# Attention forward and backward with a K/V cache: preparations moved inside the pair loop, the second phase's first operands loaded early, narrower blocks

## The chip, the cores and the metric

The kernel runs on one core of one Trainium2 chip. The time is device microseconds of that core for one execution. Comparisons are always with runs of the kernel before on the same chip in the same rounds.

The engines' short names in the profile: PE is the matmul engine (TensorE), PEld its weight loads, DVE, ACT and POOL are VectorE, ScalarE and GpSimd, SP is SyncE, which here only issues DMAs.

## The reference

```python
B, Sq, D = 16, 112, 448
H, Sk, Dh = 16, 512, 256

def _fwd_reference(x, k_cache, v_cache, wq, wo):
    q = (x @ wq).reshape(B, Sq, H, Dh).transpose(0, 2, 1, 3)
    scores = jnp.einsum("bhqd,bhkd->bhqk", q, k_cache) * (Dh ** -0.5)
    p = softmax(scores, axis=-1)
    o = jnp.einsum("bhqk,bhkd->bhqd", p, v_cache)
    return o.transpose(0, 2, 1, 3).reshape(B, Sq, H * Dh) @ wo

def reference(x, k_cache, v_cache, wq, wo, grad_out):
    out, vjp = jax.vjp(_fwd_reference, x, k_cache, v_cache, wq, wo)
    return (out, *vjp(grad_out))        # out, dx, dk_cache, dv_cache, dwq, dwo
```

All arrays are bf16. (The random inputs are cut, and the transposes are written out plainly.)

## The kernel before

Phase 1 goes over 128 pairs of heads (16 batches of 8 pairs) in a software pipeline: an iteration does the first half of pair `a` and the rest of pair `bb = a - 1`. It writes dV and dK, and it leaves O and dQ in two DRAM tiles, the stash. Phase 2a reads the stash in blocks of 512 columns for dWo (`out_5`) and dWq (`out_4`); phase 2b reads it again, transposed, in 14 chunks of rows for out and dx.

```python
    o_stash = dram.tile([B * SQ, HD], bf, name="o_stash")
    dq_stash = dram.tile([B * SQ, HD], bf, name="dq_stash")
    # ...
    def w_prep(hp):               # Wo of one pair of heads, transposed; first batch only
        # ... 2 x 8 transposes on PE, each half followed by
            nc.vector.tensor_copy(WoT_sb[...], pb[:DCH, :].rearrange(...))      # L105
    def b_prep(b):                # x and grad of one batch, transposed
        # ... 4 + 4 transposes on PE
        nc.vector.tensor_copy(xgT[:]..., pb[:DCH, :2 * DC * SQ])                # L130
    # ...
    for per in range(NPAIR + 1):
        a, bb = per, per - 1
        A, Bv = valid(a), valid(bb)
        # ... loads of K and V of the next pair
        if A:
            s_dOproj(a)           # its first matmul (L178) reads WoT_sb and xgT
            s_Qproj(a); s_T(a); s_QdT(a)
        if Bv:
            s_dV(bb); s_dST(bb)
        if A:
            s_S(a); s_dP(a)       # softmax; dP; dS on POOL
        if Bv:
            s_dK(bb); s_O(bb); s_dQ(bb)     # the last two write the stash
        if A:
            s_PT(a)
        if A:
            ba, hpa = pair_bh(a)
            if ba == 0 and hpa + 1 < HP:
                w_prep(hpa + 1)             # for the next pair
            if hpa == HP - 1 and ba + 1 < B:
                b_prep(ba + 1)              # for the next pair
    mctx.close()                  # phase 1's memory comes free
    # ... phase 2a
    load_rows(g_all, g_flat, 0, D, nc.sync)
    for blk in range(HD // 512):
        Ot = ph2.tile([P, NCH, 512], bf, name="Ot")
        load_rows(Ot, o_stash, blk * 512, (blk + 1) * 512, nc.sync)
        if blk == 0:
            load_rows(x_all, x_flat, 0, D, nc.sync)
        dQt = ph2.tile([P, NCH, 512], bf, name="dQt")
        load_rows(dQt, dq_stash, blk * 512, (blk + 1) * 512, nc.sync)
        if blk == 0:
            nc.sync.dma_start(Wo_nat[:], ...)           # 3.7 MB in one DMA
        # ... 4 groups x 14 matmuls with Ot (L436), 4 x 14 with dQt (L449)
    nc.sync.dma_start_transpose(WqT[:], wq)             # all of Wq in one DMA
    for ch, (r0, rn) in enumerate(chunks):              # phase 2b
        # ... transposed loads of the stash's rows; 32 matmuls L467, 32 of L471
    store_rows(out_flat, res_out, nc.sync)              # 1568 KB each, at the end
    store_rows(dx_flat, res_dx, nc.scalar)
```

## Time and profile before

| | before |
|---|---|
| median of 6 runs (range) | 1710.83 us (1708.72 to 1715.4) |
| span of the profiled run, PE's mean granted clock | 1710.0 us, 0.995 |
| PE busy | 1652.5 us, 97% |
| one ordinary pair / one pair that ends a batch | 9.93 us / 11.83 us |
| PE's first matmul of phase 2 | 1348.52 us |
| end of PE's last matmul | 1702.2 us |

PE is the bound, so the first view to read is the list of its waits; the prediction below shows it. A listed wait runs from the recorded end of PE's previous matmul to the start of the next. This is one batch boundary in the timeline of the kernel before (start, duration, engine, line, operation, out<-in; the two lines after these, the copy of L130 and L178, stand in the prediction):

```profile
1004.63 0.37 PE L127 MATMUL bankb<-ident_bf,g_sb 112*112 112x112 bf16 x4
...
1005.05 0.69 DVE L248 TENSOR_TENSOR O_sb<-bank,rinv 112x512 bf16<-112x512 f32 x1
```

L178 starts at 1006.32, after a listed wait of 1.32 us. Between the transposes and the copy that PE waits for stands DVE's evacuation of O.

### The profile page before, as it was taken

Reading aid. Unit: us, or ns where it says so; the run is one execution under the profiler, and the core shown is the slowest. Engines: PE = TensorE matmul, PEld = TensorE weight load, DVE = VectorE, ACT = ScalarE, POOL = GpSimd, SP = SyncE. Lnnn points to the kernel's source line nnn. Section 1 sums busy time; section 2 is a strip of 40 time slices with the busy share of each in tenths; the row PEclk is TensorE's granted clock in tenths of the full one; section 3 lists DMA queues with packets and bytes.
Section 4 is the critical chain, followed back from the end, with each engine's and each line's share of the span. In section 5 each row is a group of like instructions: output and inputs, shape, how many; then the busy total and the mean of one; then the engine's idle time right before and its main releaser. Section 6 shows DMA issues by size and latency. Waiting matters only on the chain.

```text
span 1710.0 us, 33740 instructions
## 1 busy us (share of the span) xinstructions
PE 1652.5 (97%) x11776; PEld 1271.6 (74%) x11776; DVE 968.3 (57%) x1870; ACT 979.0 (57%) x2095; POOL 719.9 (42%) x854
## 2 busy tenths in 40 slices
PE   7999999999999999999999999999999699999998
PEld 5778888888888888888888888888888455555554
DVE  4767677677676776777767777676777211110000
ACT  3667777777777777777777777777767210100000
POOL 4445554455544555445554455554555111110000
PEclk9999999999999999999999999999999899999999
DMA  9767797867776667677776667776666997618885
GB/s 261 235 220 235 241 278 237 267 228 241 229 237 230 233 229 239 229 234 229 229 239 232 232 227 238 232 238 225 231 228 225 347 317 245 213 39 172 172 173 149
DMA packets 356474, 390.40 MB, mean 228 GB/s; under 512 B 148464, under 2 KB 221728, under 8 KB 356304
## 3 DMA queue, kind: packets, MB, share of 16 engines
q1 hardware_dynamic: 348640, 371.96, 69.7%
q0 software_dynamic: 4864, 13.77, 2.5%
q10 hardware_dynamic: 2800, 2.52, 0.5%
q8 instruction: 93, 1.52, 0.4%
q14 instruction: 77, 0.63, 0.1%
HBM read 181.01 MB, written 174.13 MB: 208 GB/s over the span
## 4 chain that ended last, share of the span: by engine, by line
PE 88%; DVE 4%; issue 3%; DMA 2%; ACT 1%; POOL 1%; SPq 0%; POOLq 0%; ACTq 0%
PE bank L161 13%; PE bank L178 7%; PE bank L189 6%; PE bank L283 6%; PE bank L214 6%; PE bank L259 6%; PE bank L449 6%; PE bank L300 5%; PE bank L245 5%; PE bank L326 5%; PE bank L436 5%; PE bank L471 5%; PE bank L467 5%; PE bank L315 2%; PE bank L234 2%
## 5 line engine op out<-in xcount | busy, mean ns | idle before, releaser
L224 POOL TENSOR_SCALAR Pn<-Pu,rinv 112x512 bf16<-112x512 bf16 x256 | 173.8, 691 | 600.5 <-DVE rinv L221 591.2
L267 POOL TENSOR_TENSOR dS<-tmp,t 112x512 bf16<-112x512 f32 x256 | 325.8, 1273 | 21.2
L168 DVE COPY VT<-bank 128x512 f32<-128x512 f32 x128 | 88.5, 691 | 231.8 <-PE bank L161 231.8
L219 ACT ACTIVATE Pu<-bank,nmax 112x512 bf16<-112x512 f32 x256 | 173.5, 682 | 71.8 <-DVE nmax L217 71.7
L305 DVE CAST dk_sb<-bank 128x512 bf16<-128x512 f32 x256 | 172.8, 681 | 70.7 <-ACT Pu L219 69.9
L263 DVE CUSTOM_DVE_ANT_0 tmp<-bank,Pn 112x512 f32<-112x512 f32 x256 | 173.7, 691 | 38.9 <-POOL Pn L224 38.7
L265 POOL TENSOR_SCALAR t<-Pn,Dv 112x512 f32<-112x512 bf16 x256 | 177.1, 692 | 20.5 <-DVE Dv L263 20.1
L192 ACT ACTIVATE Q_sb<-bank 112x512 bf16<-112x512 f32 x128 | 76.4, 597 | 190.4 <-PE bank L189 190.4
L288 DVE CAST dv_sb<-bank 128x512 bf16<-128x512 f32 x256 | 165.0, 685 | 17.3 <-DMA out_dram<-dv_sb 0.8
L217 DVE TENSOR_REDUCE nmax<-bank 112x1 f32<-112x512 f32 x256 | 165.0, 686 | 1.9 <-PE bank L214 1.9
L178 PE MATMUL bank<-WoT_sb,xgT 112*112 112x512 bf16 x512 | 134.1, 382 | 25.8 <-DVE xgT L130 20.6
L161 PE MATMUL bank<-ident_f,v 128*128 128x128 f32 x1024 | 154.8, 274 | 2.0 <-DMA v<-in_v_cache_dram 2.0
L161 PE MATMUL bank<-ident_f,k 128*128 128x128 f32 x1024 | 154.8, 273 | 0.7 <-DMA k<-in_k_cache_dram 0.7
L166 ACT COPY KT<-bank 128x512 f32<-128x512 f32 x256 | 152.2, 595 | 2.0 <-PE bank L161 1.4
L161 PEld LDWEIGHTS bank<-ident_f,k 128*128 128x128 f32 x1024 | 124.6, 141 | 22.1 <-issue 1.5
L286 ACT CAST dv_sb<-bank 128x512 bf16<-128x512 f32 x256 | 138.8, 599 | 0.7 <-DMA out_dram<-dv_sb 0.6
L214 PE MATMUL bank<-KT,QdT 128*112 128x512 bf16 x512 | 137.6, 390 | 0.6 <-ACT QdT L204 0.6
L259 PE MATMUL bank<-VT,QdT 128*112 128x512 bf16 x512 | 136.9, 388 | 0.0
L303 ACT CAST dk_sb<-bank 128x512 bf16<-128x512 f32 x256 | 136.7, 592 | 0.0
L329 ACT ACTIVATE dQ_sb<-bank 112x512 bf16<-112x512 f32 x128 | 76.4, 597 | 100.3 <-PE bank L326 98.6
L189 PE MATMUL bank<-Wq_sb,xgT 112*112 112x512 bf16 x512 | 133.2, 381 | 0.0
L245 PE MATMUL bank<-v,PT 128*112 128x256 bf16 x1024 | 133.0, 272 | 0.2 <-ACT Pu L219 0.2
(64 smaller groups left out, 2879.9 us busy)
## 6 DMA issues: line engine op xcount, KB each, us to landing
k<-in_k_cache_dram SPq DMA_DIRECT2D x128, 512.0 KB, 3.9
v<-in_v_cache_dram SPq DMA_DIRECT2D x128, 512.0 KB, 4.5
out_dram<-dv_sb SPq DMA_DIRECT2D x256, 256.0 KB, 2.3
out_dram<-dk_sb SPq DMA_DIRECT2D x256, 256.0 KB, 2.3
o_stash<-O_sb SPq DMA_DIRECT2D x128, 112.0 KB, 3.0
dq_stash<-dQ_sb SPq DMA_DIRECT2D x128, 112.0 KB, 2.9
Ot<-o_stash SPq DMA_DIRECT2D x8, 1792.0 KB, 9.2
dQt<-dq_stash SPq DMA_DIRECT2D x8, 1792.0 KB, 9.3
```

The source lines that it names most:

```text
L161: nc.tensor.transpose(ps[:, s * P:(s + 1) * P], src[:, hh, s, :].bitcast(f32), ident_f[:])
L178: nc.tensor.matmul(ps_do[:SQ, :], xgT[:, 1, c, :], WoT_sb[:, c, h0 * DH:(h0 + 2) * DH], start=(c == 0), stop=(c == DC - 1))
L189: nc.tensor.matmul(ps_q[:SQ, :], xgT[:, 0, c, :], Wq_sb[:, c, h0 * DH:(h0 + 2) * DH], start=(c == 0), stop=(c == DC - 1))
L214: nc.tensor.matmul(ps_s[:SQ, :], st.QdT[:, hh, e::2], st.KT[hh][:, e::2], start=(e == 0), stop=(e == 1))
L219: nc.scalar.activation(Pu[:], ps_s[:SQ, :], ACT.Exp, bias=nmax[:], scale=1.0, accum_out=rs[:, hh:hh + 1])
L224: nc.gpsimd.tensor_scalar(Pn[:], st.Pu[hh][:], st.rinv[:, hh:hh + 1], 1.0, ALU.mult, ALU.mult)
L245: nc.tensor.matmul(ps_o[:SQ, hh * DH:(hh + 1) * DH], st.PT[:, hh * 2 + t, e2::2], st.v2[:, hh, s, :], start=(s == 0), stop=(s == NS - 1))
L259: nc.tensor.matmul(ps_dp[:SQ, :], st.QdT[:, 2 + hh, e::2], st.VT[hh][:, e::2], start=(e == 0), stop=(e == 1))
L263: nc.vector.tensor_tensor_reduce(tmp[:], ps_dp[:SQ, :], st.Pn[hh][:], 1.0, 0.0, ALU.mult, ALU.add, Dv[:])
L265: nc.gpsimd.tensor_scalar(t2[:], st.Pn[hh][:], Dv[:], -1.0, ALU.mult, ALU.mult)
L267: nc.gpsimd.tensor_tensor(dS_t[:], tmp[:], t2[:], op=ALU.add)
L305: nc.vector.tensor_copy(dk_sb[:, 2:4, :].rearrange("p s d -> p (s d)"), ps[:])
```

## The change

Its intent: PE should not wait at the batch boundaries, in the first batch, or between the phases, and the last stores should be short.

1. `b_prep` and `w_prep` move from the end of the iteration to just after the Q/dO transposes.
2. The stash is split into a tile with the rows of the first 14 batches and one with those of the last 2. x, grad and the first block's operands get memory of their own and are loaded before phase 1 ends; the first block of phase 2a works on 12 full chunks of rows first.
3. Phase 2a has one block of 512 columns and 14 of 256. Wq's transpose and Wo come in four pieces each, in blocks 3 to 10. SP's order of issues in phase 2 is as written (`manual_schedule`); before, the scheduler chose it.
4. The stores of the first 12 chunks of out and dx move ahead of the last chunk.
5. The intermediate `t2` of dS becomes bf16.

```diff
-    o_stash = dram.tile([B * SQ, HD], bf, name="o_stash")
+    BG = B - 2 if B > 2 else B
+    o_st = [dram.tile([RG, HD], bf, name="o_stash0")]
+    if BG < B:
+        o_st.append(dram.tile([(B - BG) * SQ, HD], bf, name="o_stash1"))
     # ... dq_st likewise; helpers that map rows to the two tiles
+    NE = min(RG // P, NCH)                       # 12 chunks of rows lie in the first tile
+    pre2 = ctx.enter_context(tc.tile_pool(name="pre2", bufs=1))
+    x_all, g_all, Ot0, dQt0 = ...                # tiles of pre2
+    def pre2_loads():
+        load_rows_plain(g_all, g_flat, 0, D, nc.sync)
+        load_rows_stash(Ot0, o_st, 0, 512, nc.sync, early=True, late=False)
+        load_rows_plain(x_all, x_flat, 0, D, nc.sync)
+        load_rows_stash(dQt0, dq_st, 0, 512, nc.sync, early=True, late=False)
@@
-            t2 = work.tile([SQ, SK], f32, name="t2", tag="t2", bufs=2)
+            t2 = work.tile([SQ, SK], bf, name="t2", tag="t2", bufs=2)
@@
+        if per == PRE2_PER:                      # 126
+            pre2_loads()
@@
             s_QdT(a)
+            if ba == 0 and hpa + 1 < HP:
+                w_prep(hpa + 1)
+            if hpa == HP - 1 and ba + 1 < B:
+                b_prep(ba + 1)
@@
-        if A:
-            if ba == 0 and hpa + 1 < HP:
-                w_prep(hpa + 1)
-            if hpa == HP - 1 and ba + 1 < B:
-                b_prep(ba + 1)
@@  phase 2a
+    load_rows_stash(Ot0, o_st, 0, 512, nc.sync, early=False, late=True)
+    load_rows_stash(dQt0, dq_st, 0, 512, nc.sync, early=False, late=True)
+    with tc.manual_schedule(engines={SP}):
+        blocks = [(0, 512)] + [(c0, 256) for c0 in range(512, HD, 256)]
+        for bi, (c0, cw) in enumerate(blocks):
+            # ... loads of this block's Ot and dQt (256 columns)
+            if 3 <= bi < 7:   # a quarter of WqT
+            if 7 <= bi < 11:  # a quarter of Wo_nat
+            if bi == 0 and NE < NCH:
+                pss = [bank_f32() for _ in groups]           # 8 PSUM banks
+                # all groups on chunks 0..11, then all on chunks 12, 13
@@  phase 2b
+        SPLIT = max(0, NCH - 2)
+            if ch == NCH - 1 and SPLIT > 0:
+                store_rows(out_flat, res_out, 0, SPLIT, nc.sync)
+                store_rows(dx_flat, res_dx, 0, SPLIT, nc.sync)
```

(`if` lines without a body stand for the loads that they name.)

## The prediction

> **What bounds the kernel now.** I read the busy shares first, then who waited for whom on the matmul engine (PE), then the chain that ended last, then the two places where PE is not busy.
>
> The page's busy shares, and PE's waits:
>
> ```profile
> PE 1652.5 (97%) x11776; PEld 1271.6 (74%) x11776; DVE 968.3 (57%) x1870; ACT 979.0 (57%) x2095; POOL 719.9 (42%) x854
> ...
> PE bank L178 <- DVE xgT L130: 20.6, 16, 1.3
> PE bank L436 <- issue: 11.5, 1, 11.5
> PE bankb L103 <- DMA wo_nat<-in_wo_dram: 6.4, 1, 6.4
> PE bank L178 <- DVE WoT_sb L105: 5.2, 7, 0.8
> PE bank L315 <- POOL dS L267: 2.5, 2, 1.3
> ```
>
> PE is busy 1652.5 of 1710.0 us, so only 57.5 us can come from removing waits; anything beyond must come from PE running faster. The waits name where: 20.6 us at the batch boundaries (16 waits, at most 1.3 us each), 11.5 us once before the first matmul of phase 2, 5.2 us in the first batch (7 waits), 2.5 us on the last pair's dS. The rest is the start (6.4 us and small ones) and the end.
>
> The stretches around the phase switch, in steady phase 2, and the tail (columns: stretch, length, PE, PEld, DVE, ACT, POOL busy, then granted clock, DMA share, GB/s):
>
> ```profile
> 204.00:228.00 24.00, 24.00 (x185) 19.79 (x184) 17.59 (x33) 18.37 (x41) 11.62 (x13) 1.00 1.05 269
> 1337.00:1348.50 11.50, 0.01 (x1) 0.01 (x1) 1.07 (x2) 1.56 (x3) 0.00 (x0) 0.63 0.85 273
> 1348.50:1362.00 13.50, 13.48 (x58) 6.51 (x59) 0.76 (x2) 1.06 (x2) 1.70 (x3) 0.81 1.09 369
> 1440.00:1500.00 60.00, 60.00 (x301) 33.44 (x299) 7.20 (x11) 5.53 (x10) 11.78 (x22) 1.00 0.60 194
> 1560.00:1650.00 90.00, 90.00 (x478) 46.53 (x477) 4.37 (x7) 4.26 (x8) 0.00 (x0) 1.00 0.83 174
> 1702.00:1710.00 8.00, 0.16 (x1) 0.00 (x0) 0.62 (x1) 0.00 (x0) 0.00 (x0) 0.71 0.59 201
> ```
>
> The second line is the hole between the phases: PE does nothing, and the clock falls. In the third PE is busy but at clock 0.81. The last is the tail: 8 us in which only the final stores run. Everywhere else PE is full, whatever the DMA share.
>
> One batch boundary and the end, from the timeline:
>
> ```profile
> 1005.65 0.61 DVE L130 COPY xgT<-bankb 112x896 bf16<-112x896 bf16 x1
> 1006.32 1.07 PE L178 MATMUL bank<-WoT_sb,xgT 112*112 112x512 bf16 x4 [1.32 <-DVE xgT L130]
> ...
> 1702.86 0.41 ACTq L476 DMA_DIRECT2D out_dram<-res_dx  x1
> ```
>
> The batch's transposed x and grad are made as the last work of the pair before, and the next pair's first matmul needs them: 1.32 us idle for a 0.61 us copy that sits behind other DVE work.
>
> **What the Trainium skill says.**
> - "TensorE: Matmul & The Clock Gate", section "Back-to-back issue gap": a warm matmul of N columns costs N/2.4 + 2.5 ns; for 256 that is 109.2 ns. The trace agrees for the shape that I need (128x112 stationary, 256 moving): in the chain of waits, eight matmuls of L245 take 0.88 us, then eight of L326 0.87 us, 109.4 ns each. The 512-wide L449 takes 12.09 us for 56, 215.9 ns each.
> - The same page, "Part 1: The HAM clock gate": an idle of some 3.4 us halves the clock and some 3.4 us of work restores it. The trace agrees in kind: after 11.5 us of idle the first 56 matmuls of L436 end at 1361.66, 13.14 us after their start, while later groups take 10.59 us.
> - "DMA: Bandwidth & Descriptors", "Specifications": transfers reach line rate from 512 B up. The changed loads have rows of exactly 512 B. No row of that size is in the trace before; its 1024 B rows move 194 GB/s at a share of 0.60, which extrapolates to 323 GB/s.
> - "GPSIMD Engine Reference", "3.1 Elementwise": the two-input add is bound by its two read ports. The trace agrees that one input is cheap (691 ns for Pn) and two are not (1273 ns for dS), so a bf16 t2 should change little.
>
> **The change part by part.**
>
> 1. The batch preparation moves from the end of the iteration to just after the Q/dO transposes. Its 8 transposes on PE (0.43 us) and its 0.61 us copy stay; the next pair's first matmul comes some 8 us later, so the wait goes. 15 boundaries (the sixteenth wait, 0.7 us, is at the start): -19.9 us. The moved copy now sits ahead of the dv casts and the row maximum, whose chain ends in dS; dS ends about 0.5 us before L315 reads it (998.70 against 999.23). PE is itself pushed back by the 0.43 us of transposes, so some 0.3 us of slack is left: no new wait expected.
>
> 2. The weight preparation moves likewise: 7 waits of 0.7 us, 5.2 us. Here two copies of 0.69 us enter the same chain against 0.95 us of transposes, leaving about 0.1 us. I take -4.5 us.
>
> 3. The phase switch. The stash is cut into rows of the first 14 batches and of the last 2, and x, grad and the first block's 12 full early row chunks are loaded before phase 1 ends. On its last pair PE then has 8 groups x 12 matmuls ready: 48 x 189 ns (10.59/56) + 48 x 216 ns = 19.4 us. The last stash write is issued at 1339.5 and lands 3 us later; the small late loads need some 3 us more, about 1346, before the early matmuls run out at 1337 + 19.4 = 1356. So the hole goes: -11.5 us, and with it the slow clock: 13.14 - 10.59 = -2.5 us. The independent matmuls can also fill the two waits on dS, 2.5 us; I take -1.5.
>
> 4. Phase 2's first part now has one block of 512 columns and 14 of 256. The out-5 matmuls keep number and width. The out-4 matmuls of 7 blocks double in number at half the width: 112 x 109.3 = 12.24 us instead of 12.09 us, +0.15 us for each of 7, +1.1 us. Weight loads double there, but they lie beside the matmuls, as in phase 1 at this same shape.
>
> 5. The transposed Wq arrives in four pieces in blocks 3 to 6 and Wo in four pieces in blocks 7 to 10. A 256-block takes 28 x 189 + 56 x 109.3 ns = 11.4 us on PE. It loads 1.84 MB and stores 0.46 MB: 2.3 MB at 323 GB/s are 7.1 us. A quarter of Wq adds 0.92 MB by transpose; from 174 GB/s at share 0.83 (210 GB/s at full share) that is 4.4 us, in all 11.5 of 11.4 us. Each load is issued about 17 us before its use, so four such blocks pass. Wo's blocks: 7.1 + 2.8 = 9.9 us. Expected stall: +1 us as a mean over what may happen.
>
> 6. Stores of the first 12 row chunks of out and dx move ahead of the last chunk. What is left is about 0.23 MB each; the 256 KB stores of phase 1 land in 2.3 us, the 1568 KB store at the end takes 6.0. -3.7 us.
>
> 7. t2 in bf16: POOL is 42% busy, and no PE wait but the last pair's is on it: 0.
>
> 8. Loading earlier costs DMA time elsewhere. A program position doesn't bind: the kernel before issued its first transpose of the stash, written after the whole pair loop, at 205 us. So x and grad may well be loaded near the start, where the DMA share is 0.9, and the early stash blocks soon after batch 13's rows are written. The line 204 to 228 shows such an intruder (two transposes, share 1.05) and PE at 24.00 of 24.00, so in steady state it is free; near the start I allow +2 us.
>
> Sum: -19.9 - 4.5 - 11.5 - 2.5 - 1.5 + 1.1 + 1 - 3.7 + 2 = -39.5 us. With 1710.8 us before: about 1671.5, rounded to 1672 us.
>
> **The rivals.**
> - *The 512 B rows are slow.* If they run at 200 GB/s, a block with a piece of Wq needs 2.3/0.200 + 4.4 = 15.9 us against 11.4, and one with a piece of Wo 14.3: 4 x 4.5 + 4 x 2.9 = 30 us less some 10 us of lead, 20 us of stall, and a time near 1692. For it: the share is already 1.17 between 1384 and 1408, while Wq is transposed. Against: 1024 B and 2048 B rows run at about the same rate (phase 1: 229 GB/s at 0.70), so no fixed cost per row shows. One in eight.
> - *The early loads push back phase 1.* Four loads of 1.6 MB in the one queue delay the dv and dk stores; their four buffers come round once in a pair (9.94 us), and casts that wait for a buffer would hold PSUM banks and then PE. For it: the last 17 us of phase 1 already have a DMA share near 0.9. Against: the line 204 to 228. Cost if true: 3 to 10 us, 1675 to 1682.
> - *The moved copies put a wait on dS.* Slack is only 0.5 us. If half of the 22 moved preparations cost 0.5 us, +5 us: 1677.
> - *The early matmuls take PSUM banks.* Block 0 holds 8 banks, all there are, until the late rows come. If they are placed well before the last pair, phase 1 runs short of banks. Against: PE is full in phase 1, so lower-priority work finds no place. Cost perhaps 10 us, one in twelve.
> - On the other side: all 2.5 us of dS waits filled and no cost for the loads gives about 1667.
>
> **Range and chances.** The gain is bounded by what waits there are: 20 + 5 + 11.5 + 2.5 + 2.5 + 4 = 45, so below 1664 is hardly possible. The risks all lie above. Range 1664 to 1685. The 2% line is at 1676.6 us, only some 5 us above my figure; each of the rivals alone would cross it. Faster 0.7, same 0.29, slower 0.01.
>
> **What would show it right or wrong.** PE's waits on xgT (20.6) and WoT (5.2) fall to about 1 us in total; the idle stretch before L436 vanishes and the granted clock stays 1.00 through the switch; PE's busy time stays near 1651; phase 2's 256-blocks repeat every 11.4 us; the span after the last matmul falls from 7.8 to about 4 us. Wrong would be: PE waits on Ot or dQt loads in phase 2 (512 B rows), waits on dS or on PSUM evacuations in phase 1 (moved copies, banks), casts of dv or dk that wait for stores (early loads), or a slower first 40 us.

## The result, and the profile after

| | before | after |
|---|---|---|
| median (range) | 1710.62 us (1708.58 to 1715.4), 16 runs | 1666.85 us (1664.13 to 1668.67), 8 runs |
| ratio, 95% interval | 1 | 0.9742 (0.9732 to 0.9752) |
| span of the profiled run | 1710.0 us | 1665.4 us |

A ratio here is the mean time of one kernel's fast runs over that of the other's of the same rounds, so it is not quite the ratio of the medians. The result lies 5 us below the predicted 1672 us and inside its range.

The page's busy shares of the kernel after:

```profile
PE 1647.1 (99%) x12168; PEld 1305.3 (78%) x12168; DVE 968.0 (58%) x1884; ACT 983.6 (59%) x2109; POOL 706.8 (42%) x882
```

PE does the same work in 1647.1 instead of 1652.5 us, and only 18 us of the span are left without it. PE's waits (line waited on, releaser, us in total, times, longest):

```profile
PE bankb L162 <- DMA wo_nat<-in_wo_dram: 7.7, 2, 5.1
PE bank L374 <- POOL dS L326: 2.3, 2, 1.2
...
PE bank L237 <- DVE xgT L189: 0.7, 1, 0.7
```

The 20.6 us on xgT have become 0.7 us (the one at the start), the 5.2 us on WoT and the 11.5 us between the phases are gone. The waits on dS are still there, and the start waits twice for Wo where it waited once.

A batch boundary in the timeline after:

```profile
974.84 0.37 PE L186 MATMUL bankb<-ident_bf,g_sb 112*112 112x112 bf16 x4
975.05 1.04 PE L342 MATMUL bank<-dO_sb,Pn 112*128 112x256 bf16 x8
...
981.12 1.03 PE L237 MATMUL bank<-WoT_sb,xgT 112*112 112x512 bf16 x4
```

The same four transposes take 0.21 us from start to start (975.05 - 974.84); before, 1.69 us passed until L178 (1006.32 - 1004.63). A boundary thus lost 1.48 us, not the listed 1.32. The times between pairs agree: 11.83 us before and 10.34 us after for the pair that ends a batch.

The starts of pairs in the first batch, before (pair 2, and pair 8, the first of the second batch):

```profile
38.52 0.59 PE L178 MATMUL bank<-WoT_sb,xgT 112*112 112x512 bf16 x2 [0.78 <-DVE WoT_sb L105]
...
109.48 1.07 PE L178 MATMUL bank<-WoT_sb,xgT 112*112 112x512 bf16 x4 [1.32 <-DVE xgT L130]
```

and after (pairs 2, 3 and 8):

```profile
36.89 1.03 PE L237 MATMUL bank<-WoT_sb,xgT 112*112 112x512 bf16 x4
48.83 1.03 PE L237 MATMUL bank<-WoT_sb,xgT 112*112 112x512 bf16 x4
...
102.48 1.03 PE L237 MATMUL bank<-WoT_sb,xgT 112*112 112x512 bf16 x4
```

The pairs of the first batch start every 11.82 us before and every 10.83 us after, 0.99 us less at a listed wait of 0.83. Pair 2 is an exception after: 11.94 us to the next.

The switch between the phases in the timeline after, and the windows around it (columns as in the prediction):

```profile
1303.43 0.41 PE L374 MATMUL bank<-ident_f,dS 112*128 112x112 f32 x2 [1.08 <-POOL dS L326]
...
1305.34 0.49 PE L374 MATMUL bank<-ident_f,dS 112*128 112x112 f32 x2 [1.17 <-POOL dS L326]
...
1306.69 1.91 PE L304 MATMUL bank<-v,PT 128*112 128x256 bf16 x8
1308.40 1.31 PE L385 MATMUL bank<-k,dST 128*112 128x256 bf16 x8
1309.54 9.24 PE L501 MATMUL bank<-g_all,Ot 128*128 128x448 bf16 x48
```

```profile
1302.00:1309.50 7.50, 5.25 (x32) 4.40 (x30) 3.89 (x8) 2.82 (x6) 3.12 (x4) 0.77 0.49 175
1309.50:1332.20 22.70, 22.70 (x114) 12.79 (x113) 1.87 (x3) 2.45 (x5) 1.69 (x4) 1.00 0.67 178
1337.00:1391.00 54.00, 54.00 (x406) 42.78 (x405) 7.37 (x15) 5.85 (x14) 15.66 (x29) 1.00 1.07 260
1391.00:1437.00 46.00, 46.00 (x340) 35.68 (x339) 5.90 (x12) 5.10 (x12) 12.99 (x24) 1.00 0.95 287
1661.70:1666.00 4.30, 0.00 (x0) 0.00 (x0) 0.58 (x1) 0.00 (x0) 0.00 (x0) 0.76 0.15 53
```

The 48 early matmuls follow phase 1 without a gap, at full clock. Between the two waits on dS and them lies a short stretch at clock 0.77: eight matmuls of L304 take 1.91 us where they take 1.04 elsewhere. In the third window SP issues the four pieces of Wq, in the fourth those of Wo: the DMA share is 1.07 and 0.95, and PE is full in both. (The share is the sum of the packets' times over the time of 16 engines; it can pass 1.) The last window is the tail. The transfer that ends the kernel, before and after (KB each, median us from issue to landing):

```profile
out_dram<-res_dx ACTq DMA_DIRECT2D x1, 1568.0 KB, 6.0
```

```profile
out_dram<-res_dx ACTq DMA_DIRECT2D x1, 224.0 KB, 2.1
```

PE's milestones in the two traces give the account by part:

| part | before | after | difference | predicted for it |
|---|---|---|---|---|
| start to pair 8 | 109.48 | 102.48 | -7.00 | -1.3 - 4.5 + 2 = -3.8 |
| pair 8 to pair 127 | 1210.65 | 1188.90 | -21.75 | 14/15 of -19.9 = -18.6 |
| pair 127 to phase 2's first matmul | 28.39 | 18.16 | -10.23 | -11.5 - 1.5 = -13.0 |
| phase 2a | 184.15 | 182.59 | -1.56 | -2.5 + 1.1 + 1 = -0.4 |
| phase 2b to PE's end | 169.53 | 169.5 | 0.0 | 0 |
| after PE's end | 7.8 | 3.8 | -4.0 | -3.7 |
| sum | 1710.0 | 1665.4 | -44.6 | -39.5 |

(Phase 2a ends here at the recorded end of its last matmul. The first 1.32 us boundary lies before pair 8. -39.5 is the sum of the prediction; its terms are sorted by part here.)

### The profile page after: what moved, and what is told of

It is laid out like the page before. It is cut to its first block, busy times and chain, and to the rows that moved or that the text cites. A ratio compares the mean times of both kernels' runs of the same rounds, so it can differ in the third digit from the quotient of the medians.

```text
span 1665.4 us, 34824 instructions
## 1 busy us (share of the span) xinstructions
PE 1647.1 (99%) x12168; PEld 1305.3 (78%) x12168; DVE 968.0 (58%) x1884; ACT 983.6 (59%) x2109; POOL 706.8 (42%) x882
## 3 DMA queue, kind: packets, MB, share of 16 engines
q10 hardware_dynamic: 1264, 1.15, 0.2%
## 5 line engine op out<-in xcount | busy, mean ns | idle before, releaser
L326 POOL TENSOR_TENSOR dS<-tmp,t 112x512 bf16<-112x512 f32 x256 | 297.4, 1162 | 21.3
L324 POOL TENSOR_SCALAR t<-Pn,Dv 112x512 bf16<-112x512 bf16 x256 | 177.0, 691 | 21.0 <-DVE Dv L322 20.6
L304 PE MATMUL bank<-v,PT 128*112 128x256 bf16 x1024 | 133.8, 274 | 1.1 <-ACT Pu L278 1.1
L342 PE MATMUL bank<-dO_sb,Pn 112*128 112x256 bf16 x1024 | 133.6, 274 | 0.0
L359 PE MATMUL bank<-Q_sb,dS 112*128 112x256 bf16 x1024 | 133.5, 273 | 0.0
```

Source lines behind the costliest of these rows:

```text
L324: nc.gpsimd.tensor_scalar(t2[:], st.Pn[hh][:], Dv[:], -1.0, ALU.mult, ALU.mult)
L326: nc.gpsimd.tensor_tensor(dS_t[:], tmp[:], t2[:], op=ALU.add)
```

## The experiments

Twelve kernels ran, in four groups, each group on one chip with its own runs of the kernel before; all gave correct results. A difference from the kernel before is worked out as (ratio - 1) x 1710 us, and its interval from that of the ratio. Differences between two experiments of one call are differences of their ratios.

| run | what it is | median us | ratio to before (95%) |
|---|---|---|---|
| e1_bprep | before, batch preparation moved | 1687.49 | 0.9874 (0.9861 to 0.9888) |
| e2_wprep | before, weight preparation moved | 1705.48 | 0.998 (0.9966 to 0.9994) |
| e3_narrow | before, 16 blocks of 256 | 1723.38 | 1.0086 (1.0072 to 1.0099) |
| e10_preps_back | after, both preparations back | 1695.17 | 0.9916 (0.9903 to 0.9929) |
| after_again | after, unaltered | 1665.93 | 0.9743 (0.973 to 0.9757) |
| e4_late_xg | after, x and grad loaded later | 1662.7 | 0.9726 (0.9713 to 0.9739) |
| e8_fill | after, early matmuls in the dS waits | 1662.54 | 0.9722 (0.9709 to 0.9735) |
| e9_late_fill | e4 and e8 together | 1659.03 | 0.9705 (0.9687 to 0.9723) |
| e5_one_store | after, final stores not split | 1672.02 | 0.9773 (0.9756 to 0.9791) |
| e6_t2_f32 | after, t2 in f32 | 1667.29 | 0.9751 (0.9734 to 0.9768) |
| e7_no_early | after, no chunk early | 1729.42 | 1.0114 (1.0098 to 1.013) |
| e11_late_block0 | after, first block loaded late | 1676.28 | 0.9805 (0.9791 to 0.9818) |

The main theory was that each gain is a removed wait of PE, as predicted, and that the excess came from losses which the listed waits understate. The rivals, run by run, put gains or costs elsewhere.

### The moved batch preparation (e1_bprep)

```diff
             s_QdT(a)
+            ba, hpa = pair_bh(a)
+            if hpa == HP - 1 and ba + 1 < B:
+                b_prep(ba + 1)
 # ... and taken out at the end of the iteration
```

> The kernel before with one thing changed: the batch preparation (transposes of x and grad and their copy) sits after the Q/dO transposes. Theory A, as in the prediction: the 15 boundary waits of 1.32 us that the profile lists go and nothing else, -19.9 us, 1690.8. Theory B, read from the two traces since: a boundary costs more than its listed wait[...]; the pair before a boundary took 11.83 us in the kernel before and 10.35 in the changed one, so -1.48 x 15 = -22.2 us, 1688.5. Rival: the moved copy delays the row maximum and dS, and some of the wait comes back as PE waits on dS: less than -17 us.

Measured: -21.5 us (-23.8 to -19.2). PE's waits of this kernel:

```profile
PE bank L437 <- issue: 11.5, 1, 11.5
...
PE bank L178 <- DVE xgT L130: 0.7, 1, 0.7
```

The wait on xgT is gone and the hole between the phases stays. The interval holds both the listed 19.9 us and 15 x 1.48 = 22.2 us, so the time alone does not decide between them. The trace does: from pair 8 to pair 127 this kernel takes 1188.92 us, as after (1188.90), against 1210.65 before. Of these 21.7 us, 20.8 lie in the 14 pairs that end a batch and 0.7 in the 15 that follow a boundary (9.98 us each before, 9.93 here); the rest is the difference of a few single pairs. The moved copy puts no wait on dS anywhere: the rival that feared it falls.

### The moved weight preparation (e2_wprep)

```diff
             s_QdT(a)
+            ba, hpa = pair_bh(a)
+            if ba == 0 and hpa + 1 < HP:
+                w_prep(hpa + 1)
 # ... and taken out at the end of the iteration
```

> The kernel before with only the weight preparation of the first batch moved. Theory A, as predicted: -4.5 us from the 7 waits on WoT (5.2 us listed), 1706. Theory B, from the traces since: the pairs of the first batch shorten by 0.99 us each (6 of them, -5.9), and the transposes also fill PE's waits at the start, so that the slow clock ends earlier (first to second pair 12.9 us in the changed kernel, 16.9 before): -10 us in all, 1700.7. Rival: the single weight buffer is now asked for earlier than its load arrives, and PE waits on that load: about 0.

Measured: -3.4 us (-5.8 to -1.0). The waits on WoT are gone, and pairs 2 to 6 take 10.83 us each as after, 0.99 us less than before: 5.0 us. The preparation now asks for Wo's slice sooner, and a new wait shows in this kernel's timeline:

```profile
27.66 1.10 PE L103 MATMUL bankb<-ident_bf,wo_nat 128*112 128x128 bf16 x16 [2.00 <-DMA wo_nat<-in_wo_dram]
```

So about 2 us are given back, which brings the 5 us near what was timed. The profiled run of this kernel started pair 8 at 100.64 us, 8.8 us before the profiled run of the kernel before. That is more than the change can account for: the start differs by several us from run to run, so a single span decides nothing below some 3 us.

### Both preparations put back (e10_preps_back)

```diff
             s_QdT(a)
-            # w_prep, b_prep
 # ...
         if Bv:
             del sts[bb]
+        # w_prep, b_prep as in the kernel before
```

> The changed kernel with both preparations put back to the end of the iteration; the rest of the change stays. If the parts are additive and the waits are all that the move removes: theory A +24.4 us on the changed kernel (1691), theory B +28 to +32 us (1695 to 1699), of which the boundaries are 22.2. If the early loads of x and grad interact with the moved weight preparation at the start (they collide there: PE waits 2.6 us on a weight load at 28 us), less comes back than e1 and e2 gained together.

Measured: 0.9916, against 0.9742 for the kernel after: +29.7 us (the two ratios are from different calls; after_again has 0.9743). In PE's waits 20.6 us on xgT return, and 4.8 us on WoT:

```profile
PE bank L237 <- DVE xgT L189: 20.6, 16, 1.3
```

The listed waits sum to 25.4 us, short of what was timed. With the losses from start to start it is 15 x 1.48 + 7 x 0.99 = 29.1 us; the spans of the two profiles differ by 28.4 us (1693.8 against 1665.4). So the moved preparations are two thirds of the whole gain, and they are worth more than the list of waits says. In the kernel before, e1 and e2 gained 24.9 us together. Each of these figures is uncertain by some 3 us, so whether the moves are worth more in the changed kernel is not shown.

### Narrow blocks alone (e3_narrow)

```diff
-    NBLK = HD // 512
+    NBLK = HD // 256
 # ... Ot, dQt and their matmuls 256 columns wide; order of loads and pieces of Wq, Wo as before
```

> The kernel before with all of phase 2's blocks 256 columns wide instead of 512 (16 blocks), nothing else. As predicted: 8 x 0.15 = +1.2 us of matmul time, loads of 512 B rows keep up: 1712. Rival of the prediction: 512 B rows are slow and PE waits on loads: +20 us or so, 1730. What the run shows also is the DMA share and rate of such rows in a stretch without other transfers: 323 GB/s at full share if a row has no fixed cost.

Measured: +14.7 us (+12.3 to +16.9), near what the rival "512 B rows are slow" had said. But its mechanism is not the one in the trace. PE's waits of this kernel, its first two groups of phase 2, then two windows, then two lines of SP's timeline:

```profile
PE bank L449 <- DMA dQt<-dq_stash: 10.9, 2, 8.4
PE bank L436 <- DMA Ot<-o_stash: 10.5, 2, 6.2
```

```profile
1332.13 5.46 PE L436 MATMUL bank<-g_all,Ot 128*128 128x448 bf16 x28
1346.01 7.79 PE L449 MATMUL bank<-dQt,x_all 128*112 128x256 bf16 x56 [8.42 <-DMA dQt<-dq_stash]
```

```profile
1337.00:1380.00 43.00, 28.41 (x190) 21.68 (x188) 3.58 (x7) 2.74 (x7) 7.09 (x13) 0.84 1.15 307
1441.00:1543.00 102.00, 102.00 (x752) 79.18 (x751) 13.28 (x27) 11.50 (x27) 28.87 (x54) 1.00 0.63 181
```

```profile
1336.17 5.98 SPq L432 DMA_DIRECT2D Wo_nat<-in_wo_dram  x1
...
1362.37 20.07 SPq L459 DMA_TRANSPOSE WqT<-in_wq_dram  x1
```

The +14.7 us is a net. Between the first matmul of phase 2 and the first of phase 2b pass 211.70 us, against 183.99 before: 27.7 us more. But the first matmul of phase 2 follows phase 1 without a gap (16.74 us after pair 127's start, 28.39 before), since the block's 256 columns of O were loaded at 1321.64 us, ahead of the last writes to the stash; a part of the old hole returns as the 8.42 us on dQt. So with one stash tile, too, a first load can come before the last write to the stash; whether the change needs its split of the stash was not tried.

All these waits on block loads lie before 1441 us, where the whole of Wo, the whole transpose of Wq and the first transposed chunks run among the block loads, at a DMA share of 1.15 (307 GB/s) in the first window; the transpose also holds SP for 20.07 us, and the next block's load is issued after it. Later the same 256-wide blocks are loaded alone and PE is full, at a DMA share of 0.63. At full share, by an estimate from this window, 512 B rows would move 181 / 0.63 = 287 GB/s, against 323 for the 1024 B rows of the kernel before: about a tenth dearer, not the 200 GB/s of the rival. The reading is that a 256-block gives PE 11.4 us of cover instead of 22.7 while the big transfers keep their size. In the kernel after, Wq and Wo come in quarters, at chosen places, and PE does not wait for the same rows. Which of the three (quarters, the fixed order on SP, the early first block) cures it was not separated.

### The same kernel again (after_again)

No edit; it anchors the next three.

> The changed kernel once more, unaltered, as the yardstick for the three runs beside it on the same chip: 1667 us, ratio 0.974.

Measured: 0.9743, as before (0.9742). Its trace has the same waits of 1.08 and 1.17 us on dS, but the eight matmuls of L304 after them take 1.04 us and not 1.91. Of eight profiled kernels that keep these two waits (1.19 and 1.28 us in e6), four (after, e5, e7, e10) had the slow stretch and four (after_again, e4, e6, e11) had none. Among the four traces with the waits of the kernel before (1.2 and 1.3 us), e1 has one too (1.85 us). So it comes and goes from trace to trace, with and without the change.

### x and grad loaded in mid phase 1 (e4_late_xg)

```diff
+        with tc.issue_after(marks[0]):        # SP: behind the V load of pair 24
             load_rows_plain(g_all, g_flat, 0, D, nc.sync)
 # ...
+        with tc.issue_after(marks[1]):        # SP: behind the V load of pair 40
             load_rows_plain(x_all, x_flat, 0, D, nc.sync)
```

The scheduler of the kernel after had issued these two loads at 19.0 and 22.9 us, because nothing holds them back; each took 20 us to land among the first loads of K, V and weights, and the issue of the second held SP for 9.66 us.

> The changed kernel, with the loads of all of x and grad queued behind loads of pairs 24 and 40 instead of at 19 and 23 us; the order of instructions on every other engine is the same. My theory: in the changed kernel these two 1.6 MB loads hold up the weight load and the stores at the start (the second pair takes 15.5 us and the third 11.9 instead of 10.8): -5.8 us, 1661. Rival: the second pair is slow because the weight preparation was moved ahead of a load into a single buffer, and the early loads have no part: 0, 1667. Second rival: the loads cost as much where they go now: 0 in time, but with waits at pair 24 and 40.

Measured: 0.9726 against 0.9743, -2.9 us, half of what was expected; each of the two ratios is known to about 2.2 us, so the time alone is weak evidence. The starts of pairs 2, 3 and 8 in this kernel:

```profile
33.32 1.03 PE L243 MATMUL bank<-WoT_sb,xgT 112*112 112x512 bf16 x4
44.14 1.03 PE L243 MATMUL bank<-WoT_sb,xgT 112*112 112x512 bf16 x4
...
97.79 1.03 PE L243 MATMUL bank<-WoT_sb,xgT 112*112 112x512 bf16 x4
```

Pair 2 now takes 10.82 us like its neighbours. Pair 8 starts at 97.79 here and at 100.17 in e9; in the seven profiled kernels with moved preparations and early loads it starts between 101.26 and 104.09, on average 102.7. Six of those seven list a wait of PE on a cast of dv, 0.5 to 6.3 us; e4 and e9 list none. e10, with the early loads but the preparations at their old place, lists such a wait as well (3.1 us), so it does not come from the moved preparations. So the early loads do cost some 3 us, and this wait fits the collision with the dv stores that a rival of the prediction named. The rest of the start, the wait of 2 us on Wo's slice, stays here too and is not theirs. Where the loads go now, PE is full in both windows (40.00 of 40 us and 50.00 of 50).

### Early matmuls ahead of the dS waits (e8_fill), and both (e9_late_fill)

```diff
         if Bv:
             s_dV(bb)
+            if not A:
+                early_groups(2)      # two of block 0's groups on its 12 early chunks
             s_dST(bb)
```

In the kernel after, the early matmuls stand behind all of the last pair's in PE's order, so they cannot fill its waits. Here two groups (24 matmuls) are written ahead of them. e9 adds the edit of e4.

> The changed kernel with 24 of the first block's 96 early matmuls (4.5 us of work, two groups) placed ahead of the last pair's dS transposes. The changed kernel idles 1.08 and 1.17 us there, and its clock then falls, so that the eight matmuls of L304 take 1.71 us instead of 0.88. My theory: the waits (2.25 us[...]) and the slow clock (1.4 us) go: -3.5 us. Rival: the fall of the clock is bound to something else than these waits: -2.3. Second rival: the held PSUM banks or the later stash writes cost it all: 0.

Measured: 0.9722 against 0.9743, -3.6 us. PE's timeline of e8_fill:

```profile
1300.64 4.71 PE L136 MATMUL bank<-g_all,Ot 128*128 128x448 bf16 x24
1305.19 0.55 PE L385 MATMUL bank<-ident_f,dS 112*128 112x112 f32 x4
```

The transposes of dS follow without a wait. 2.25 us of waits are saved. From the start of pair 127 to the first matmul of phase 2b it takes 196.2 us in the profiles of e8 and e9, 198.9 in that of after_again: 2.7 us. The rest of the 3.6 us is within the noise of the timing. Neither profile has a slow stretch, but 7 of the 12 with the waits have none either, so that this goes with the waits is not shown.

> Both of the above together, which touch different ends of phase 1. If additive: -9 us against the changed kernel, 1658, the fastest of all; with only one of them real, 1661 to 1664.

Measured: 0.9705 (0.9687 to 0.9723), median 1659.03 us: -6.5 us against after_again, which is what the two give by themselves (2.9 + 3.6), with 3 us of uncertainty. This is the lowest median of all, 0.4% under the kernel after; its interval overlaps those of e4 and e8.

### The final stores in one piece (e5_one_store)

```diff
-        SPLIT = max(0, NCH - 2)
+        SPLIT = 0
```

> The changed kernel with out and dx stored whole at the end, as the kernel before does. Predicted effect of the split 3.7 us; the traces since show the stretch after the last matmul fall from 7.8 to 3.8 us: +4 us, 1671. Rival: the early stores slow down the last transposes or the end of PE's work, and the net is less: +2.

Measured: 0.9773, +5.3 us against the kernel after (0.9742). It was run at another time. In the trace 7.8 us pass after PE's end, as before, against 3.8: 4.0 us. The step holds; the rest is within the intervals.

### t2 in f32 (e6_t2_f32)

```diff
-            t2 = work.tile([SQ, SK], bf, name="t2", tag="t2", bufs=2)
+            t2 = work.tile([SQ, SK], f32, name="t2", tag="t2", bufs=2)
```

> The changed kernel with t2 in f32 again. Predicted effect of bf16: none, since no PE wait but the last pair's is on POOL. Expected 0 to +0.3 us (the dS add goes from 1162 back to 1273 ns, twice on the last pair). Rival: dS has only half a microsecond of slack after the moved copies, and the 0.11 us per add was needed: PE waits on dS appear at boundaries, +2 us or more.

Measured: 0.9751, +1.5 us against the kernel after, with intervals that overlap: no difference shown. bf16 does make the add on POOL faster. The groups of dS in the kernels before (f32) and after (bf16):

```profile
L267 POOL TENSOR_TENSOR dS<-tmp,t 112x512 bf16<-112x512 f32 x256 | 325.8, 1273 | 21.2
```

```profile
L326 POOL TENSOR_TENSOR dS<-tmp,t 112x512 bf16<-112x512 f32 x256 | 297.4, 1162 | 21.3
```

But only the last pair's dS is waited for, so 0.11 us is saved twice: e6's two waits are 1.19 and 1.28 us instead of 1.08 and 1.17. No boundary waits on dS in e6 either, so the moved preparations did not need the faster add.

### No chunk early (e7_no_early): an experiment that missed

```diff
-    NE = min(RG // P, NCH)
+    NE = 0
```

> The changed kernel without early rows of the stash: all 14 row chunks of the first block are loaded after the last pair's stash write, so that nothing is ready for PE when phase 1 ends; x and grad are still there early. My theory: the hole of 11.5 us before phase 2 and 2.5 us of slow clock after it come back: +12 to +14 us, 1680. Rival: the hole came mainly from the loads of x, grad and Wo, which stay out of the way here: +6 us or less.

Measured: 1.0114, +63.6 us against the kernel after. It does not say what it was meant to say. The first block's loads still came before phase 1's end (1088 to 1248 us), now as small DMAs, and there was no hole. But with NE at 0 every later block is loaded with 15 small DMAs for each stash as well. A line of SP's timeline:

```profile
1328.37 7.09 SPq L121 DMA_DIRECT2D Ot<-o_stash  x15
```

7.0 to 9.1 us of issuing for each half of a block is 14 to 16 us for a block that PE works through in 11.4. PE then waits on Ot 24.5 us, on dQt 6.5 and on the transposed chunks 6.8. An issue of a small DMA cost 7.09 / 15 = 0.47 us of SP. It took another experiment to measure the early loads.

### The first block loaded after phase 1 (e11_late_block0)

```diff
-        load_rows_stash(Ot0, o_st, 0, 512, nc.sync, early=True, late=False)    # in pre2_loads, dQt0 too
 # ...
-    load_rows_stash(Ot0, o_st, 0, 512, nc.sync, early=False, late=True)
-    load_rows_stash(dQt0, dq_st, 0, 512, nc.sync, early=False, late=True)
+    with tc.issue_after(last_write[0]):       # SP: behind the last write to the stash
+        load_rows_stash(Ot0, o_st, 0, 512, nc.sync)
+        load_rows_stash(dQt0, dq_st, 0, 512, nc.sync)
```

> The changed kernel with all of the first block's stash loads queued behind the last pair's stash writes, where the kernel before has them; x and grad stay early, Wo and Wq stay in later blocks. (The run without early rows did not do this: its loads still came 60 us before the end of phase 1, since the first block's columns are written by the first pair of each batch.) My theory: the time of that load is the hole. 1.8 MB took 8.2 us there in the kernel before; PE then waits about 11 us before its first matmul of phase 2 and runs some 2.5 us behind at the low clock: +11 to +14 us on the changed kernel, 1678. Rival: the hole was long because x, grad and 3.7 MB of Wo were loaded in the same stretch; with these gone it shrinks to half: +5 to +7, 1672.

Measured: 0.9805, +10.8 us against the kernel after, just under the 11 to 14 expected and well above the rival's 5 to 7. It was run at another time. PE's timeline of this kernel:

```profile
1314.62 11.19 PE L504 MATMUL bank<-g_all,Ot 128*128 128x448 bf16 x48 [8.90 <-DMA Ot<-o_stash]
```

The hole is back with 8.90 us, and with it a slow clock: the next group starts 11.03 us later where the kernel after needs 9.08, 1.95 us more. Together 10.85 us, which is what was timed. The hole of the kernel before was 11.5 us: there the same load was issued at 1340.25 us, behind the last writes to the stash, and landed at 1348.43, and PE began at 1348.52. Here x, grad, Wo and Wq stay out of the way; the difference of the two holes was not tried further.

## Why the prediction was right

The direction, the size and the range were right. The bound "below 1664 is hardly possible" was wrong: it summed the listed waits, and e4, e8 and e9 have medians of 1662.7, 1662.5 and 1659.0 us. By its own steps:

- **What bounds it** held: PE's waits were what there was to win, and they went. PE's busy time was said to stay near 1651 us and is 1647.1.
- **Step 1, boundaries**: right mechanism, mis-sized term. -19.9 us was the sum of listed waits; from start to start a boundary loses 1.48 us, 22.2 us for 15, and e1 timed 21.5. The wait on dS that it feared did not come (e1, e6).
- **Step 2, weights**: -4.5 us. The pairs show -5.0 us in pairs 2 to 6, e2 timed -3.4; a new wait of 2 us on Wo's slice, which the step had not thought of, takes part of it back.
- **Step 3, the switch**: -14 us for hole and slow clock. Before, 28.39 us pass from pair 127 to phase 2, in after_again 16.50 (1290.81 to 1307.31), in the profiled run of the kernel after 18.16 because of the slow stretch; there the clock did not stay at 1.00 through the switch, as the prediction had it. So -11.9 us for the hole, and -2.5 for the clock (56 matmuls from start to start: 13.14 us before, 9.08 + 1.52 after): right, and in e11 10.8 us come back with the late loads of the first block. The detail was wrong: the prediction had the late rows land about 1346 us, just in time. The first block's 512 columns are those of each batch's first pair of heads, so its last rows are complete at pair 120; they were loaded at 1247.5 us, 62 us before phase 2 and 81 us before PE's first matmul with them (1328.98).
- **The failed term of step 3** is "the independent matmuls can also fill the two waits on dS", -1.5 us. PE's waits stayed at 1.08 and 1.17 us, since the early matmuls stand behind the last pair's. e8 puts them ahead, and gains 3.6 us as timed, 2.7 of them at the switch in the traces.
- **Steps 4 and 5, blocks**: a 256-block takes 11.41 us, as predicted. +1.1 us for the narrower matmuls holds (phase 2a: -2.5 + 1.1 = -1.4, measured -1.56), and the +1 us of stall did not come. The prediction did not name the fixed order of SP as a part of the change. e3 shows that it, or the pieces, matters: with the scheduler's order and whole Wq and Wo such blocks make phase 2a 27.7 us longer. The rival's reason (slow rows) was wrong; that its 20 us are near e3's net of 14.7 is luck. The formula that the prediction took from "Back-to-back issue gap" stands there for isolated matmuls, and the section has about 131 ns for 512 columns in a stream with weight loads; the 215.9 ns of the trace fit the formula.
- **Step 6, tail**: -3.7 us predicted, -4.0 in the trace, 5.3 us timed by e5 with some 3 us of uncertainty.
- **Step 7, t2**: 0 holds within what can be timed (e6).
- **Step 8, early loads**: "+2 us near the start", measured about 3 (e4). The loads were indeed hoisted to the start.

The sum was 5 us short of the -44.6 us in the traces. By the table of parts, 3.2 us of it lie in the start and 3.2 in the boundaries, 1.2 in phase 2a; the switch gave 2.8 us less in that profile. Of the start's 3.2 us only part is explained: it differs by several us from run to run, so that the single profile of the kernel before (109.48 at pair 8; e3, with the same start, has 105.99, and e1 104.15 + 1.48 = 105.6) flatters the change there.

Open are the exact share of the start that is not due to the early loads, which of pieces, order and early block spares the kernel after the stalls of e3, and whether the split of the stash is needed.

## What to carry to other kernels

Read what a wait costs from start to start of the matmuls around it, beside the same work without a wait; each listed wait was 0.16 us short here (1.32 for 1.48, 0.83 for 0.99). Work that the next iteration's first instruction needs should stand several microseconds before the iteration's end, and independent matmuls fill a wait only if they stand before it in the engine's order. A load that nothing holds back may be issued at the very start of the program, where it is dearest: tie it to a point where the DMAs have room. A block that covers half as long may need its big transfers cut as well; e3 suggests it and does not prove it.

## What the Trainium skill lacked or had wrong

- "TensorE: Matmul & The Clock Gate", Part 1, tells of a slow clock after an idle window of about 3.4 us. Here two idles of 1.1 to 1.3 us, 2 us apart, were followed by a slow stretch (eight matmuls in 1.76 to 1.91 instead of 1.04 us) in five of twelve profiled kernels and not in the others; that the idles cause it is not shown. The page says the window runs free and that the cold start varies; its section on a second failure mode tells of micro-idles between groups of matmuls, without their length. After one idle of 8.90 us the loss was 1.95 us, after 11.5 us 2.5 us.
- "DMA: Bandwidth & Descriptors", "Specifications", gives 512 B as the size from which transfers reach line rate. Rows of 512 B came to 287 GB/s at full share (181 at 0.63), rows of 1024 B to 323 (194 at 0.60). Both are estimates from windows that also hold the blocks' stores, but the smaller is about a tenth dearer. The page's section "Why small descriptors are slow" has a fixed overhead for each packet, which points the same way.
- The same page, "Anatomy of one DMA", has some 50 ns for the sequencer's dispatch on the GpSimd path. On SP an issue was recorded with 0.33 to 0.47 us, and 15 of them with 7.09 us; in e7, with a DMA share of 0.63 between 1330 and 1400 us, that bound the blocks and cost 63.6 us in all. For the sequencer's time on SP's path the page has 512 cycles for each DMA of "previous generations"; that stands in its part on trn3 B0 and gives no time.
- "GPSIMD Engine Reference", "3.1 Elementwise", explains the two-input add by its two reads and gives f32. With one of the two inputs in bf16 the 112x512 add took 1162 instead of 1273 ns, 9% less.
